# Chunked attention and a low-rank mixer on one core: side work on VectorE's queue re-spaced, transposes bound to their block, and early buffers taken from one ring of eight

## The chip, the core and the metric

The kernel runs on one core of a Trainium2 chip. A core has TensorE (PE; its weight loads are shown as PEld), VectorE (DVE), ScalarE (ACT), GpSimd (POOL) and SyncE (SP), and 16 DMA engines that they share. Each engine works through its own queue strictly in order and waits on semaphores for the others. The metric is device time in microseconds (us) of one execution, the median of several.

## The reference

```python
def _attn_ref(q, k, v):                       # (8, 8, 576, 64) each: batch, heads, rows, head width
    q_c, k_c, v_c = (a.reshape(B, H, 9, 64, D) for a in (q, k, v))
    scores = (1 / sqrt(D)) * np.matmul(q_c, k_c.transpose(0, 1, 2, 4, 3))
    attn = softmax(scores)                    # with the row maximum taken off first
    return np.matmul(attn, v_c).reshape(B, H, S, D)

def _moe_ref(x, U, V, w_ch1, w_ch2):          # x: (8, 576, 512), the attention's output, heads side by side
    h = x.transpose(0, 2, 1) @ U @ V          # rank 32, mixes the 576 rows
    u = x + h.transpose(0, 2, 1)
    return u + np.maximum(u @ w_ch1, 0.0) @ w_ch2    # 512 -> 2048 -> 512
```

The weights U, V, w_ch1 and w_ch2 arrive as 8-byte floats; the rest is fp32.

## The kernel before

**Tiles.** Two batches make a pair (pr = 0 to 3), 1152 rows, cut into nine tiles of 128 rows (t = 0 to 8). Three tiles make a group (g = 0 to 2).

**The main work.** For each pair and group, the channel product runs in 16 blocks f = 0 to 15, each over 128 of the 2048 hidden channels. `hidden` (L744) makes h in 12 matmuls of 384 columns; `relu_high` (L759, ACT) writes hh, the high part of relu(h); `relu_low` (L764, DVE) writes hl, the rest; `project_out` (L771) adds hh and hl times the second weight into o, 9 matmuls of 512 columns per block. TensorE's queue holds the `hidden` of a block ahead of the o of the block before it, sometimes two ahead. There are 192 such blocks.

**The lead-in.** Until the first block can run, the kernel turns the 8-byte weights into fp32 pairs (`rounding`, `splitting`: ACT and DVE), does the attention of pair 0's nine tiles, projects them with U (`project_ops`, y), with V (`mix_ops`, u), and transposes the sum (ut). This part and the first 32 blocks (groups 0 and 1 of pair 0) are ordered by a planner, `order` (L147), from costs and from counts of buffers, `ROOM`. V goes through `v_ops` (L273): loaded to `vraw`, rounded in `vroom` by six DVE steps (L94 to L103), written to DRAM as `vrows` (POOL queue, L290), read back four times as `vall` (POOL queue, L295), then split into `vst` by ACT (L298) and DVE (L303). The v rows of each early tile (`qkv_t`) are also loaded from POOL's queue.

**The steady part.** From pair 0, group 2 on, side work for the next tiles is called from a list of words (`LATER`, `FIRST`, L951) spread evenly over the 4 places of each of the 16 blocks, but for the last `TAIL` places. The words: `t` the two transposes of q and k of a tile, `s` its scores and softmax, `q` the transpose of the softmax's result, `l`, `f`, `u` the three steps of the mixer for a tile, `p` a projection step, `h` one strided copy of q or k within DRAM (halfq, halfk), `.` nothing. Where a word is called doesn't fix where its instructions stand: the framework's scheduler puts each engine's instructions in order by its own estimate, within the data dependencies.

**Transposes through DMA and DVE.** From pair 1's tile 2 on no TensorE transpose is used. q and k come by one DMA in 32-row blocks (qn, kn; L417) and are turned by DVE block transposes into qT and kT (`squares`, L480). The softmax result ex is written to DRAM (es_td, L459), read back (es, L400) and turned into eT (`square_e`, L539). The mixer's x goes the same way: us_td (L454), us (L400), uT (`square_u`, L709). scores (sc) read qT and kT; `values` (av) reads eT; ACT and DVE split uT into uth and utl, the next group's input.

**Buffers.** `slot` (L71) gives out buffers by tag: three of "qk", two of "vn", one each of "e", "eT", "us", "uT". The early tiles take ex from "qk" and eT from "eT", "us", "uT" in turn (L467); the last three weights' rooms take `XTAGS` (L53). The load of a tile (`load`, L446) is called in the word `s` of the tile before it, right behind that tile's scores (L941 to L945).

Of the kernel before, what the change touches and what calls it, by code (L numbers as in the profile page):

```python
# [12 lines left out]
U32 = mybir.dt.uint32  # L13
# [8 lines left out]
def kernel(  # L22
# [29 lines left out]
    XROOM = 3  # L52
    XTAGS = (("qk", "us"), ("qk", "uT"), ("qk", "e"))  # L53
    BLOCKS = [(hp, e, c) for hp in range(HP) for e in range(2) for c in range(2)]
# [13 lines left out]
    def bank(name):  # L68
        return psum.tile([P, 512], F32, tag="bank", name=name)

    def slot(tag, dtype, name, shape=(P, 512)):  # L71
        return work.tile(list(shape), dtype, tag=tag, name=name, bufs=SLOTS[tag])

# [48 lines left out]

    ROOM = {"bank": 8, "w": NF, **SLOTS, "x": NX, "y": 2, "ut": 2, "h": 2, "mx": 2, "sm": 2}
    COLD = 1.0
# [197 lines left out]
    def w_ops(f, after=None):  # L322
        st = {}

        def load():
            raw = wslot((2 * DM, 2), U32, f"wraw_{f}")
            nc.sync.dma_start(
                raw[:, 0:DM].rearrange("p (cc f) w -> p cc (f w)", cc=NCC),
                moe_w_ch1[:, 2 * f * P : 2 * (f + 1) * P].rearrange("(cc p) f -> p cc f", p=P),
            )  # L330
            nc.sync.dma_start(raw[:, DM:].rearrange("p c w -> p (c w)"), moe_w_ch2[f * P : (f + 1) * P, :])
            st["raw"] = raw

        n = 1 if f < NF - XROOM else 2
        size = 2 * DM // n
        ld = Op("SP", 3.2, load, after, take="w", lat=2.0)
        halves = []
        for z in range(n):
            cols = slice(z * size, (z + 1) * size)

            def room(z=z):
                return wslot((size,), U32, f"wroom_{f}") if n == 1 else slot(XTAGS[f - NF][z], U32, f"wroom_{f}_{z}")

            def high(v, cols=cols):
                if cols.start == 0:
                    del st["raw"]
                    w = st["w"] = wslot((2, 2 * DM), F32R, f"w_{f}")
                    w1[f] = w[:, :, 0:DM].rearrange("p s (c f) -> p s c f", c=NCC)
                    w2[f] = w[:, :, DM:]
                nc.scalar.copy(st["w"][:, 0, cols], v)  # L350

            def low(v, cols=cols):
                nc.vector.tensor_sub(st["w"][:, 1, cols], v, st["w"][:, 0, cols])

            raw = Later(lambda cols=cols: st["raw"][:, cols])
            tag = "w" if n == 1 else XTAGS[f - NF][z]
            halves.append((*rounding(raw, room, ld, tag, size), high, low, tag))
        rounded = [h[0] for h in halves]
        return [splitting(r, high, low, rounded, tag, size) for _, r, high, low, tag in halves]
# [90 lines left out]
    def put(src, name, by_channel=False):  # L450
# [9 lines left out]
        return kept  # L460

    def attention_ops(pr, t, *after):
        n = f"{pr}_{t}"
        st = {}
        mine = early(pr, t)
        own = plain(pr, t)
        tag_e, tag_eT = ("qk", ("eT", "us", "uT")[t % 3]) if mine else ("e", "eT")  # L467

# [9 lines left out]
        def squares(z, name):  # L478
            dst = slot("qk", F32, name + n, (P, HP, P))
            nc.vector.transpose(  # L480
                dst.rearrange("p h (n j a) -> p n a h j", n=2, j=SQ),
                loaded[pr, t][z].rearrange("p (n a) (h i) -> p n a h i", n=2, i=SQ),
            )
            st[name] = dst
# [52 lines left out]
        def square_e():  # L537
            st["eT_"] = slot("eT", F32, "eT_" + n, (P, HP, P))
            nc.vector.transpose(  # L539
                st["eT_"].rearrange("p h (j a) -> p a h j", j=SQ), st["es"].rearrange("p a (h i) -> p a h i", i=SQ)  # L540
# [136 lines left out]
    def mix_ops(pr, t, x, ys, after=None, first=None):  # L677
# [29 lines left out]
        def square_u():  # L707
            uT = st["t"] = slot("uT", F32, "uT_" + n)
            nc.vector.transpose(  # L709
                uT.rearrange("p (c j a) -> p a c j", c=NCC, j=SQ), st["us"].rearrange("p a (c i) -> p a c i", i=SQ)  # L710
# [124 lines left out]
    GATES = (28, 30)  # L835
    TAIL = 8
    HALVES_FROM = 13
# [90 lines left out]

    def begin_next(i):
        if i + 1 < len(tiles) and tiles[i + 1] not in loaded:  # L930
            load(*tiles[i + 1])

    def attend(pr, t, what):
# [9 lines left out]
        done = behind.pop(0)[2] if len(behind) > 1 else []  # L943
        i = tiles.index((pr, t))
        return [*done, soft[0], lambda: begin_next(i), *soft[1:]]  # L945

    def do(group):
# [3 lines left out]
    LATER = {  # L951
# [3 lines left out]
    }  # L955
    FIRST = "t2 s2 p0 p1 h h t3 q2 s3 p2 h . h t4 q3 s4 p3 h . t5 h q4 s5 p4 . l0 . f0 l1 . . u0 f1 l2 . . u1 f2 . . . u2"

# [7 lines left out]
    def go(pr, g, word):  # L965
        if word == ".":
            return
        if word == "h":
            if to_halve:
                to_halve.pop(0)()  # L970
            return
        kind, i = word[0], int(word[1:])
        if kind in "tsqa":
            at = pr + 1 if g else pr
# [66 lines left out]
```

## Time and profile before

| | |
|---|---|
| time, median of 3 runs | 1000.47 us (999.69 to 1002.86) |
| the profiled execution: its time, its span in the trace | 1000.45 us, 998.6 us |
| TensorE busy / weight loads / DVE / ACT | 944.5 / 821.2 / 486.7 / 213.2 us |
| granted TensorE clock, mean | 0.98 |
| first matmul of the first block | at 70.8 us |

All positions are us from the span's start. In a row of the timeline stand start, length, engine, line, operation, output<-input with shapes, the count of instructions merged, and in brackets how long the engine sat idle before and what ended that. "SPq" and "POOL ... DMA_DIRECT2D" rows are issues of DMAs; their length is the time to issue. A row of the table by windows gives busy time and count of PE, PEld, DVE, ACT, POOL, then the granted clock (1.00 is full), the DMA share and GB/s. A row of the waits gives total, times and longest, in us. "issue" as a releaser means that the profile shows nothing that was waited for.

### The profile page before, as it was taken

What the parts mean: (1) busy time and instruction counts of PE and PEld (TensorE: products, weight loads), DVE (VectorE), ACT (ScalarE), POOL (GpSimd) and SP (SyncE); (2) the same over time, 40 slices, a digit from 0 to 9 for tenths busy, and PEclk for the clock granted to TensorE, in tenths of its full rate; (3) what the DMA queues carried; (4) which work ended last, traced back from release to release, by engine and by line L of the source; (5) the groups of instructions that cost most, each with busy time, mean ns of one, the idle gap of its engine ahead of it and who ended that gap; (6) DMA issues with size and microseconds to landing.
All of it is one profiled execution on the core that took longest, in us unless ns stands there. A gap on an engine that the chain in (4) does not pass through costs nothing.

```text
span 998.6 us, 16154 instructions
## 1 busy us (share of the span) xinstructions
PE 944.5 (95%) x6660; PEld 821.2 (82%) x6663; DVE 486.7 (49%) x915; ACT 213.2 (21%) x385; POOL 33.8 (3%) x89
## 2 busy tenths in 40 slices
PE   7969999998998999999999799999999999999998
PEld 4648999877797888888898689787888788899997
DVE  5869999673544534443544443453443553421211
ACT  4433433231111212111211111111111121111110
POOL 6510000000000000000000000000000000000000
PEclk8979999999999899999999899999999999999999
DMA  9952178657526524544643632663231412210000
GB/s 223 246 150 81 53 179 189 98 148 147 129 61 141 110 63 102 120 96 106 131 86 75 132 76 43 140 128 88 83 81 39 125 45 43 75 22 1 32 1 32
DMA packets 272152, 97.80 MB, mean 98 GB/s; under 512 B 224192, under 2 KB 258016, under 8 KB 272080
## 3 DMA queue, kind: packets, MB, share of 16 engines
q1 hardware_dynamic: 270560, 93.61, 41.4%
q0 software_dynamic: 1520, 3.17, 1.4%
q8 instruction: 52, 0.85, 0.4%
q14 instruction: 20, 0.16, 0.0%
HBM read 73.61 MB, written 37.30 MB: 111 GB/s over the span
## 4 chain that ended last, share of the span: by engine, by line
PE 72%; DMA 13%; SPq 5%; DVE 5%; issue 2%; ACT 2%; POOL 1%; DVEq 0%; POOLq 0%; ACTq 0%
PE o L779 32%; PE h L752 32%; SPq L438 3%; DMA kn<-halfk 2%; PE av L550 2%; PE sc L502 1%; DVE eT L539 1%; SPq L454 1%; DMA es_2d<-ex 1%; PE u L687 1%; DMA us_3d<-x 1%; DMA es<-es_2d 1%; DMA us<-us_3d 1%; SPq L417 1%; DMA vall<-vrows 1%
## 5 line engine op out<-in xcount | busy, mean ns | idle before, releaser
L752 PE MATMUL h<-uth,w 128*128 128x384 f32 x1536 | 413.2, 339 | 0.0
L779 PE MATMUL o<-w,hh 128*128 128x512 f32 x1152 | 357.8, 400 | 3.3 <-ACT hh L761 3.3
L752 PEld LDWEIGHTS h<-uth,w 128*128 128x128 f32 x1536 | 281.5, 188 | 8.6
L752 PE MATMUL h<-utl,w 128*128 128x384 f32 x768 | 259.8, 338 | 0.0
L779 PEld LDWEIGHTS o<-w,hh 128*128 128x128 f32 x1152 | 214.4, 190 | 43.2 <-ACT hh L761 5.3
L779 PE MATMUL o<-w,hl 128*128 128x512 f32 x576 | 219.6, 402 | 3.5 <-DVE hl L766 3.3
L766 DVE SCALAR_TENSOR_TENSOR hl<-h,hh 128x384 fp32r<-128x384 f32 x192 | 104.9, 551 | 209.7 <-ACT hh L761 209.2
L761 ACT ACTIVATE hh<-h 128x384 fp32r<-128x384 f32 x192 | 93.8, 490 | 437.1 <-PE h L752 436.9
L752 PEld LDWEIGHTS h<-utl,w 128*128 128x128 f32 x768 | 144.5, 188 | 7.1
L779 PEld LDWEIGHTS o<-w,hl 128*128 128x128 f32 x576 | 108.8, 190 | 33.1 <-DVE hl L766 7.7
L539 DVE STREAM_TRANSPOSE eT<-es 128x512 f32<-128x512 f32 x25 | 27.4, 1096 | 84.1 <-DMA es<-es_3d 14.6
L709 DVE STREAM_TRANSPOSE uT<-us 128x512 f32<-128x512 f32 x27 | 29.6, 1097 | 60.9 <-DMA us<-us_2d 12.6
L719 ACT CAST uth<-uT 128x512 fp32r<-128x512 f32 x27 | 16.8, 620 | 124.5 <-DVE uT L709 124.5
L693 DVE TENSOR_TENSOR x<-u,x 128x512 f32<-128x512 f32 x36 | 24.1, 682 | 32.6 <-PE u L687 32.5
L531 ACT ACTIVATE ex<-ex 128x512 f32<-128x512 f32 x36 | 22.7, 632 | 79.3 <-DVE ex L523 72.8
L480 DVE STREAM_TRANSPOSE kT<-kn 128x512 f32<-128x512 f32 x25 | 17.8, 712 | 41.2 <-DMA kn<-halfk 41.2
L550 PEld LDWEIGHTS av<-vn,eT 64*64 64x64 f32 x864 | 17.3, 133 | 25.0 <-issue 25.0
L550 PE MATMUL av<-vn,eT 64*64 64x65 f32 x864 | 21.9, 224 | 13.5 <-DVE eT L539 8.8
L636 ACT CAST xh<-x 128x512 fp32r<-128x512 f32 x30 | 18.6, 619 | 61.4 <-DVE x L569 55.5
L516 DVE TENSOR_REDUCE mx<-sc 128x4 f32<-128x256 f32 x72 | 28.0, 416 | 4.9 <-PE sc L502 4.8
L414 POOL MEMSET vn<- 128x8 f32 x27 | 3.0, 114 | 737.1 <-PE av L550 720.7
L569 DVE TENSOR_TENSOR x<-av,sm 128x256 f32<-128x256 f32 x72 | 27.2, 419 | 1.2
(95 smaller groups left out, 562.3 us busy)
## 6 DMA issues: line engine op xcount, KB each, us to landing
wraw<-in_moe_w_ch_dram SPq DMA_DIRECT2D x32, 512.0 KB
out_dram<-x SPq DMA_DIRECT2D x36, 256.0 KB
halfq<-in_q_dram SPq DMA_DIRECT2D x24, 288.0 KB
halfk<-in_k_dram SPq DMA_DIRECT2D x24, 288.0 KB
vn<-in_v_dram SPq DMA_DIRECT2D x108, 64.0 KB
qn<-halfq SPq DMA_DIRECT2D x25, 256.0 KB
kn<-halfk SPq DMA_DIRECT2D x25, 256.0 KB
qkv<-in_v_dram POOLq DMA_DIRECT2D x36, 64.0 KB, 6.0
```

What stands on the lines that cost most here:

```text
L438: d = queue.dma_start(vn[e * C : (e + 1) * C, c, :, 0:D], v[b, heads(pr, t, e), s0 : s0 + C, :].rearrange("h s d -> s h d"),)
L516: nc.vector.reduce_max(mx, st["sc"][e], axis=AX.X)
L531: nc.scalar.activation(exf, exf, AF.Exp, scale=SCALE)
L539: nc.vector.transpose(st["eT_"].rearrange("p h (j a) -> p a h j", j=SQ), st["es"].rearrange("p a (h i) -> p a h i", i=SQ))
L550: nc.tensor.matmul(ps[e][cs, hp * D1 : (hp + 1) * D1], lhsT=st["eT_"][rows, hp, cs], rhs=vn[rows, c, hp, :], start=True, stop=True,)
L569: nc.vector.tensor_mul(by_head[:, heads(pr, t, e), :], st["av"][e][:, :, 0:D], st["sm"][:, e].unsqueeze(2).broadcast_to([P, HP, D]),)
L693: nc.vector.tensor_add(x, st["u"], x)
L709: nc.vector.transpose(uT.rearrange("p (c j a) -> p a c j", c=NCC, j=SQ), st["us"].rearrange("p a (c i) -> p a c i", i=SQ))
L752: o = nc.tensor.matmul(ps[:, :GN], lhsT=w[:, z, cc], rhs=u[:, cc, :], start=(n == 0), stop=(n == 3 * NCC - 1))
L761: nc.scalar.activation(hh, ps[:, :GN], AF.Relu)
L766: nc.vector.scalar_tensor_tensor(hl, ps[:, :GN], 0.0, hh, op0=ALU.max, op1=ALU.subtract)
L779: nc.tensor.matmul(acc[g, j], lhsT=h[:, js], rhs=w2[f][:, z], start=(first and i == 0), stop=(final and i == 2),)
```

## The change

Four things are changed. (1) In the planned part, the early tiles' ex and eT and the last three weights' rooms take a buffer from one ring of eight in a fixed turn (`RING`), and the planner counts them as one stock "slot" of eight. (2) Every DVE block transpose gets an added dependency on the last matmul of the `hidden` issued last when it is called (`square`), so that the scheduler can't set it ahead of that block. (3) Loads of tiles leave the word `s` and get a word of their own, `n`, with numbers from 9 on meaning the next pair. (4) The lists are spaced anew, and `TAIL` is 6 in place of 8: 58 of 64 places are used, not 56.

```diff
-    XTAGS = (("qk", "us"), ("qk", "uT"), ("qk", "e"))
+    RING = ("qk", "qk", "qk", "e", "eT", "us", "uT", "vn")
...
+    turn_of = itertools.cycle(RING)
+
     def slot(tag, dtype, name, shape=(P, 512)):
+        tag = next(turn_of) if tag == "slot" else tag
         return work.tile(list(shape), dtype, tag=tag, name=name, bufs=SLOTS[tag])
...
-    ROOM = {"bank": 8, "w": NF, **SLOTS, "x": NX, "y": 2, "ut": 2, "h": 2, "mx": 2, "sm": 2}
+    ROOM = {"bank": 8, "w": NF, **SLOTS, "slot": len(RING), "x": NX, "y": 2, "ut": 2, "h": 2, "mx": 2, "sm": 2}
...
-                return wslot((size,), U32, f"wroom_{f}") if n == 1 else slot(XTAGS[f - NF][z], U32, f"wroom_{f}_{z}")
+                return wslot((size,), U32, f"wroom_{f}") if n == 1 else slot("slot", U32, f"wroom_{f}_{z}")
...
+    def square(dst, src):
+        turned = nc.vector.transpose(dst, src)
+        sync = mybir.DependencyInfo(mybir.DependencyClass.Sync, mybir.DependencyReason.DATA)
+        tc.add_manual_dep(turned.ins, hidden_last[-1].ins.name, sync, reason="not before this block")
...
-        tag_e, tag_eT = ("qk", ("eT", "us", "uT")[t % 3]) if mine else ("e", "eT")
+        tag_e, tag_eT = ("slot", "slot") if mine else ("e", "eT")
...
-            nc.vector.transpose(
+            square(
...
-    TAIL = 8
+    TAIL = 6
...
-        i = tiles.index((pr, t))
-        return [*done, soft[0], lambda: begin_next(i), *soft[1:]]
+        return [*done, *soft]
...
     LATER = {
-        0: "t6 q5 s6 l3 h f3 h t7 q6 s7 u3 p0 p1 h t8 h q7 s8 p2 p3 h . . q8 a8 p4 . l4 . f4 l5 . . u4 f5 . . . u5",
+        0: "t6 q5 s6 l3 n7 h f3 t7 q6 s7 u3 n8 p0 h t8 q7 s8 p1 n9 h p2 h q8 a8 p3 h p4 . l4 . f4 l5 . u4 f5 . u5",
...
+        if kind == "n":
+            key = pr + (g > 0) + i // NT, i % NT
+            if key[0] < NPAIR:
+                load(*key)
+            return
```

The three calls of `nc.vector.transpose` (L480, L539, L709 before) all go through `square`. The line numbers of the changed kernel are higher by up to 9, so L480, L539 and L709 are one line there, L467.

**VectorE, pair 1, group 0, blocks 1 to 3.** qT_7 and kT_7 are the transposes of tile 7, eT_6 that of tile 6's softmax, uT_3 that of tile 3's x; hl_0_f is the low part of block f of group 0. Before:

```order
L480 STREAM_TRANSPOSE qT_7_3196<-qn_7_3106 128x2x2x4x32
L523 TENSOR_TENSOR ex_6_3116<-sc_1_6_3088,mx_6_3117 128x4x2x32
L523 TENSOR_TENSOR ex_6_3116<-sc_1_6_3089,mx_6_3117 128x4x2x32
L791 TENSOR_TENSOR x_8_772<-o_8_2382,x_8_772 128x512
L480 STREAM_TRANSPOSE kT_7_3198<-kn_7_3107 128x2x2x4x32
L693 TENSOR_TENSOR x_3_2587<-u_3_3149,x_3_2587 128x512
L766 SCALAR_TENSOR_TENSOR hl_0_1_3147<-h_0_1_3132,hh_0_1_3145 128x384
L766 SCALAR_TENSOR_TENSOR hl_0_2_3187<-h_0_2_3172,hh_0_2_3185 128x384
L539 STREAM_TRANSPOSE eT_6_3203<-es_6_3125 128x4x128
L709 STREAM_TRANSPOSE uT_3_3292<-us_3_3170 128x4x128
L766 SCALAR_TENSOR_TENSOR hl_0_3_3220<-h_0_3_3205,hh_0_3_3218 128x384
```

and now:

```order
L532 TENSOR_TENSOR ex_6_3113<-sc_1_6_3095,mx_6_3114 128x4x2x32
L578 TENSOR_TENSOR x_5_3092<-av_1_5_3070,sm_5_3088 128x256
L578 TENSOR_TENSOR x_5_3092<-av_1_5_3071,sm_5_3088 128x256
L532 TENSOR_TENSOR ex_6_3113<-sc_1_6_3096,mx_6_3114 128x4x2x32
L702 TENSOR_TENSOR x_3_2615<-u_3_3141,x_3_2615 128x512
L775 SCALAR_TENSOR_TENSOR hl_0_1_3139<-h_0_1_3124,hh_0_1_3137 128x384
L467 STREAM_TRANSPOSE qT_7_3197<-qn_7_3157 128x2x2x4x32
L775 SCALAR_TENSOR_TENSOR hl_0_2_3187<-h_0_2_3172,hh_0_2_3185 128x384
L467 STREAM_TRANSPOSE kT_7_3199<-kn_7_3158 128x2x2x4x32
L467 STREAM_TRANSPOSE eT_6_3221<-es_6_3122 128x4x128
L467 STREAM_TRANSPOSE uT_3_3286<-us_3_3192 128x4x128
L775 SCALAR_TENSOR_TENSOR hl_0_3_3219<-h_0_3_3204,hh_0_3_3217 128x384
```

The pair qT_7, kT_7 stood inside and behind tile 6's softmax and ahead of hl_0_1; now each stands one block later, qT_7 behind hl_0_1 and kT_7 behind hl_0_2. eT_6 and uT_3 stand ahead of hl_0_3 as before.

**SyncE, the same place.** kn_7 is tile 7's load of k, es_6d and es_6 are the store and the read-back of tile 6's softmax, us_3d and us_3 those of tile 3's x. Before:

```order
L417 DMA kn_7_3107<-halfk_1574 128x2x256
L438 DMA vn_7_3108<-in_v_dram 64x4x64 x2
L794 DMA out_dram<-x_8_772 128x512
L459 DMA es_6d<-ex_6_3116 128x4x128
L389 DMA halfk_2641<-in_k_dram 9x256x32
L454 DMA us_3d<-x_3_2587 128x4x32 x3
L400 DMA es_6_3125<-es_6d 128x512
L454 DMA us_3d<-x_3_2587 128x4x32
L417 DMA qn_8_3265<-halfq_1400 128x2x256
L400 DMA us_3_3170<-us_3d 128x512
```

and now:

```order
L803 DMA out_dram<-x_8_775 128x512
L421 DMA kn_7_3158<-halfk_1574 128x2x256
L442 DMA vn_7_3159<-in_v_dram 64x4x64 x3
L458 DMA us_3d<-x_3_2615 128x4x32
L463 DMA es_6d<-ex_6_3113 128x4x128
L458 DMA us_3d<-x_3_2615 128x4x32 x3
L404 DMA es_6_3122<-es_6d 128x512
L404 DMA us_3_3192<-us_3d 128x512
L421 DMA qn_8_3312<-halfq_1442 128x2x256
```

The strided copies halfk have left this stretch, the store us_3d begins ahead of es_6d, and us_3 follows es_6 with nothing between.

**GpSimd's queue in the lead-in.** Rows qkv_t load the v rows of early tile t. Before:

```order
L438 DMA qkv_2_347<-in_v_dram 64x4x64 x4
L414 MEMSET qkv_8_500 128x8
L438 DMA qkv_5_434<-in_v_dram 64x4x64 x4
L290 DMA vrows<-vroom 128x144
L438 DMA qkv_8_500<-in_v_dram 64x4x64 x4
L414 MEMSET qkv_6_636 128x8
L295 DMA vall<-vrows 32x576 x4
L414 MEMSET qkv_7_706 128x8
L438 DMA qkv_6_636<-in_v_dram 64x4x64 x4
```

and now:

```order
L442 DMA qkv_2_347<-in_v_dram 64x4x64 x4
L418 MEMSET qkv_8_483 128x8
L294 DMA vrows<-vroom 128x144
L442 DMA qkv_5_432<-in_v_dram 64x4x64 x4
L299 DMA vall<-vrows 32x576 x4
L442 DMA qkv_8_483<-in_v_dram 64x4x64 x4
L418 MEMSET qkv_6_622 128x8
L418 MEMSET qkv_7_682 128x8
L442 DMA qkv_6_622<-in_v_dram 64x4x64 x4
```

vrows is now ahead of tile 5's loads and vall ahead of tile 8's. On VectorE the six steps on vroom are now in one piece, where before the last three stood behind the softmax of tile 2 and the end of tile 4.

More of the change, by code (lines that the diff above doesn't have):

```diff
@@ L1 @@
+import itertools
 import math
@@ L355, in w_ops @@
             raw = Later(lambda cols=cols: st["raw"][:, cols])
-            tag = "w" if n == 1 else XTAGS[f - NF][z]
+            tag = "w" if n == 1 else "slot"
             halves.append((*rounding(raw, room, ld, tag, size), high, low, tag))
@@ L538, in square_e @@
             st["eT_"] = slot("eT", F32, "eT_" + n, (P, HP, P))
-            nc.vector.transpose(
+            square(
                 st["eT_"].rearrange("p h (j a) -> p a h j", j=SQ), st["es"].rearrange("p a (h i) -> p a h i", i=SQ)
@@ L708, in square_u @@
             uT = st["t"] = slot("uT", F32, "uT_" + n)
-            nc.vector.transpose(
+            square(
                 uT.rearrange("p (c j a) -> p a c j", c=NCC, j=SQ), st["us"].rearrange("p a (c i) -> p a c i", i=SQ)
@@ L927 @@
     behind = []
-    def begin_next(i):
-        if i + 1 < len(tiles) and tiles[i + 1] not in loaded:
-            load(*tiles[i + 1])
     def attend(pr, t, what):
@@ L951 @@
     LATER = {
[3 rows of a table removed]
[3 rows of a table added]
     }
-    FIRST = "t2 s2 p0 p1 h h t3 q2 s3 p2 h . h t4 q3 s4 p3 h . t5 h q4 s5 p4 . l0 . f0 l1 . . u0 f1 l2 . . u1 f2 . . . u2"
+    FIRST = "p0 p1 h t2 s2 n3 h . t3 . q2 s3 p2 n4 h h . t4 . q3 s4 p3 n5 h . t5 . q4 s5 h n6 p4 . l0 . f0 l1 . u0 f1 l2 . u1 f2 . . u2"
     def plan():
```

4 rows, old and new, of the table LATER are left out of this document.

## The prediction

> **What bounds the kernel now.** I read the table by windows first, to see where TensorE stands still, then the waits of TensorE, then the timeline at one long stop, then the clock.
>
> ```profile
> 78.00:200.00 122.00, 121.77 (x613) 109.96 (x611) 109.98 (x148) 44.12 (x65) 0.00 (x0) 1.00 0.54 115
> 200.00:994.00 794.00, 762.56 (x5259) 670.74 (x5259) 322.87 (x639) 134.80 (x260) 2.81 (x25) 0.99 0.37 84
> ```
>
> TensorE is the bound: of the 122 us from 78 to 200 it idles 0.2. From 200 on it idles 794 - 762.56 = **31.4 us**, and more in the lead-in ahead of 78. VectorE, busy 323 of those 794 us, isn't full; it is late at certain points. The waits of TensorE from 200 to 830:
>
> ```profile
> PE y L647 <- ACT xh L636: 9.8, 3, 3.9
> PE av L550 <- DVE eT L539: 8.8, 5, 3.4
> PE av L550 <- issue: 4.6, 3, 2.3
> ```
>
> The columns are total, times, longest. These rows name 23.2 of the 31.4 us: products of y and av that wait for data which came through DMA and a VectorE transpose. Most of the rest are o products behind hh and hl, which queue behind such a transpose. The timeline of the stop near 320 us (pair 1, group 0) shows how: VectorE, ScalarE, SyncE's queue and TensorE.
>
> ```profile
> 305.89 0.75 DVE L516 TENSOR_REDUCE mx<-sc 128x4 f32<-128x256 f32 x2
> 306.56 0.70 DVE L480 STREAM_TRANSPOSE qT<-qn 128x512 f32<-128x512 f32 x1
> 307.18 0.71 DVE L523 TENSOR_TENSOR ex<-sc,mx 128x256 f32<-128x256 f32 x2
> ...
> 311.57 0.71 DVE L480 STREAM_TRANSPOSE kT<-kn 128x512 f32<-128x512 f32 x1 [3.08 <-DMA kn<-halfk]
> ...
> 319.38 1.08 DVE L539 STREAM_TRANSPOSE eT<-es 128x512 f32<-128x512 f32 x1 [5.59 <-DMA es<-es_6d]
> 322.24 1.08 DVE L709 STREAM_TRANSPOSE uT<-us 128x512 f32<-128x512 f32 x1 [1.79 <-DMA us<-us_3d]
> 323.18 0.54 DVE L766 SCALAR_TENSOR_TENSOR hl<-h,hh 128x384 fp32r<-128x384 f32 x1
> ```
>
> ```profile
> 307.93 0.63 ACT L531 ACTIVATE ex<-ex 128x512 f32<-128x512 f32 x1 [5.17 <-DVE ex L523]
> ```
>
> ```profile
> 308.42 0.60 SPq L417 DMA_DIRECT2D kn<-halfk  x1
> ...
> 311.07 0.38 SPq L459 DMA_DIRECT2D es_6d<-ex  x1
> ...
> 316.36 0.47 SPq L400 DMA_DIRECT2D es<-es_6d  x1
> ...
> 319.75 0.33 SPq L400 DMA_DIRECT2D us<-us_3d  x1
> ```
>
> ```profile
> 320.55 0.70 PE L550 MATMUL av<-vn,eT 64*64 64x65 f32 x32 [1.52 <-issue]
> ...
> 325.40 0.80 PE L647 MATMUL y<-xh,ust 128*128 128x512 f32 x1 [3.69 <-ACT xh L636]
> ```
>
> The scores of tile 6 reach VectorE at 305.89. The transpose qT of the next tile is set into the softmax, then kT stands 3.08 us for a load issued at 308.42, and all behind it is late: the add to x that us_3d stores, so that the store, the read-back issued at 319.75 and uT (322.24) slip. The softmax, ready at 308.56, is stored only at 311.07, behind kn and vn on SP's queue, and read back at 316.36. So eT ends at 320.46, 14.6 us after the scores came; av waits 1.52 us and y 3.69. The row of y counts three such stops, one for each pair that has a next one.
>
> ```profile
> DVE kT L480 <- DMA kn<-halfk: 41.2, 21, 5.7
> ```
>
> Waits for kn were 21, with 41.2 us, most of them hidden by the `hidden` that TensorE runs ahead.
>
> **The change part by part.** Steady part, idle time. No transpose and no DMA is added or taken away. The added dependency makes a transpose wait for the `hidden` of its block; hl of that block can't start before that either, and in the new order none stands ahead of the hl of an earlier block, so the wait by itself costs nothing. I walked the place above through the new order with the rows' durations, and these of the chain of waits:
>
> ```profile
> 78.78 4.22 PE h L752 x24
> 83.00 4.18 PE o L779 x18
> ...
> 229.98 3.05 DMA es_2d<-ex
> 233.04 2.55 DMA es<-es_2d
> ```
>
> A block's 12 h are 2.11 us, its 9 o 2.09. From the end of tile 6's scores to its av TensorE now has three blocks of these, u (a matmul of an o's size, 0.2) and six more o (1.4): 14.2 us; before it was 13.5, with the stop of 1.52 behind. VectorE does the maxima and differences without qT between (0.3 + 0.75 + 0.71, and 0.8 for the scaling of tile 5 among them), exp takes 0.63, the store waits for one issue of us_3d on SP (0.5), is issued (0.38) and lands (3.05), the read-back takes 2.55, eT 1.08: 10.8 us, 3.4 ahead of av. uT_3, whose store is no longer behind a kT, ends at about 14.9, hl_0_3 at 15.5; it is wanted at 17.5, and y, placed one h later than before, at 18. So the 5.2 us of this place go, and those of its two likes. For av of tiles 2 and 8 the same count gives 13.0 and 11.8 us from scores to av where it gave 11.4 and 9.6, against stops of 8.8 us in five, the longest 3.4. The o rows go with the kT that leaves their way. What I leave: three places in each of three pairs have under 1 us of room by the same walk (eT_7, eT_8, uT_5); with 0.8 us each and some contention that is **8 us**. So 31.4 - 8 = **23.4 us less**. Bounds: 31.4 less; or, if all 41.2 us of the kT row came through to TensorE, 41.2 - 31.4 = 9.8 more.
>
> Steady part, clock. The windows behind the stops, and one with a shorter stop:
>
> ```profile
> 236.00:242.00 6.00, 5.04 (x76) 4.66 (x77) 4.81 (x13) 1.25 (x2) 0.11 (x1) 0.72 0.64 114
> 321.00:327.00 6.00, 2.31 (x55) 1.89 (x45) 3.71 (x9) 1.85 (x3) 0.11 (x1) 0.70 0.76 160
> 327.00:333.00 6.00, 6.00 (x25) 5.21 (x24) 3.48 (x8) 1.08 (x3) 0.00 (x0) 0.73 0.38 103
> 560.00:566.00 6.00, 3.68 (x9) 3.00 (x10) 4.95 (x14) 1.85 (x3) 0.00 (x0) 0.52 0.61 120
> 796.00:802.00 6.00, 3.96 (x10) 2.91 (x11) 5.07 (x14) 2.40 (x5) 0.00 (x0) 0.72 0.36 87
> 676.00:686.00 10.00, 7.88 (x96) 6.57 (x95) 2.25 (x6) 0.98 (x2) 0.09 (x1) 1.00 0.27 80
> ```
>
> The granted clock is the figure behind POOL's count. Busy time times what is missing: 5.04 x 0.28 + 2.31 x 0.30 + 6.00 x 0.27 + 3.68 x 0.48 + 3.96 x 0.28 = **6.6 us**. The last row holds a stop of 2.1 us at 1.00. I take the loss to shrink as the long stops do: 5.6 of 6.6 us go; bounds 0 and 6.6. The Trainium skill (TensorE: Matmul & The Clock Gate, What's actually happening) says the clock falls to half only after an idle window of about 3.4 us; by it none would be left with stops under 1 us, which is 1 us less than my sum.
>
> Lead-in: VectorE on V, POOL's queue, ScalarE, TensorE, and the windows.
>
> ```profile
> 32.05 0.31 DVE L98 SCALAR_TENSOR_TENSOR vroom<-vraw,vroom 128x144 uint32<-128x144 uint32 x1
> ...
> 36.38 0.23 DVE L101 TENSOR_SCALAR vraw<-vroom 128x144 uint32<-128x144 uint32 x1
> ...
> 36.99 0.31 DVE L103 TENSOR_TENSOR vroom<-vroom,vraw 128x144 f32<-128x144 f32 x1
> ```
>
> ```profile
> 37.59 0.56 POOL L290 DMA_DIRECT2D vrows<-vroom  x1 [3.47 <-DVE vroom L103]
> ...
> 44.19 1.03 POOL L295 DMA_DIRECT2D vall<-vrows  x2 [3.41 <-issue]
> 45.40 1.46 POOL L295 DMA_DIRECT2D vall<-vrows  x2 [0.18 <-issue]
> ```
>
> ```profile
> 53.87 0.67 ACT L298 CAST vst<-vall 128x576 fp32r<-128x576 f32 x1 [7.35 <-DMA vall<-vrows]
> ```
>
> ```profile
> 58.59 2.05 PE L687 MATMUL u<-ys,vst 128*128 128x512 f32 x4 [7.27 <-DVE vst L303]
> ```
>
> ```profile
> 50.00:58.00 8.00, 1.33 (x7) 0.50 (x5) 1.83 (x4) 3.44 (x6) 2.61 (x6) 0.73 1.09 272
> 58.00:64.00 6.00, 5.41 (x60) 4.14 (x64) 3.88 (x7) 1.27 (x3) 0.00 (x0) 0.50 0.24 67
> ```
>
> V's rounding is split: its first three steps end at 32.36, its last three (36.38 to 37.30, 0.9 us) stand behind other work. vrows is issued at 37.59, the read-back vall from 44.19 to 46.86, it lands at 53.85, and TensorE stands 7.3 us; then the clock is 0.50 with 5.41 us busy, 2.7 us lost. Now the six steps are in one piece and end at 32.36 + 0.9 = 33.3. vrows goes there and lands some 3.6 us later (0.56 to issue, 3.05 as the stores above); vall, behind tile 5's loads alone, is issued from 36.9 to 39.5 and with the same 7 us lands at about **46.5**, 7.3 us earlier. What is late next is VectorE: it was idle 8.00 - 1.83 and 6.00 - 3.88, together 8.3 us, from 50 to 64, and needs perhaps 2.3 of it still for the chain from scores over softmax to av of tiles 6 and 7. So **6 us less**; bounds 0 and 8.3. That passes on only as far as VectorE's weight steps come earlier too, since it is busy 110 of 122 us from 78 to 200; they stand behind the same hole, so I take it whole. The ring costs no instruction; what it frees (the rooms of the last weights) lies where TensorE has 0.2 us to win.
>
> The wider spacing puts the last u of a group later; its uT must end ahead of the next group's first h. By the lengths above that chain is 10 us (add 0.7, four stores 2, landing 3, read-back 2.9, turn 1.1), and by the order it has 14 or more: nothing.
>
> **Sum.** From the span 998.6: - 23.4 - 5.6 - 6.0 = 963.6; the execution took 1.85 us more than its span (1000.45, the median to 0.02 us), so 965.5, **966 us**.
>
> **The rivals.** The stops move. The stores and read-backs keep their length, and half of the 23.2 us of av and y stays beside my 8, that is 11.6 us, with 3 us of the clock: 966 + 14.6 = **980 us**. For it: the room found is 1 to 4 us, and every landing in it is from one execution. Against it: no transpose stands inside a softmax any more. Chance 0.20.
>
> The lead-in doesn't gain. vall then starts among the loads for which the DMA column shows 1.09 up to 58, and lands no earlier than they let it: 966 + 6 = **972 us**. For it: that column is 0.24 only from 58 on, just behind vall's landing. Against: the same 7 us were measured among those loads. Chance 0.10. The Trainium skill speaks for this rival (DMA: Bandwidth & Descriptors, Issuing engines are not separate DMA queues): what POOL issues runs on the same 16 DMA engines as what SP issues, and another queue saves only the time to issue.
>
> Slower. A load now goes out one block (4.2 us) ahead of its turn, not two, since `n` stands a word or more behind `s`. Should kn land behind its own block's hh, VectorE stands at kT ahead of the hl that TensorE wants next, with nothing run ahead to hide it. For 24 tiles this decides from 35.0 / 24 = 1.5 us per tile on; with 1.8, below the 41.2 / 21 = 2.0 that VectorE stood there on average, the time is 966 + 43 = **1009 us**. Against it: kn is issued about 2.2 us behind the scores and lands 3.7 later (0.60 + 3.08), at 6; kT of tile 7 stands behind hl_0_2, at 8. Chance 0.07.
>
> No change. The order moves, but av, y and o wait for the same last DMAs and the lead-in for its weights: **998 us**, 0.05.
>
> **How the numbers follow.** My forecast has 0.58; its own range is 958 to 974. With the first two rivals that is 0.88, so the range goes from 955 (all terms at their better bounds: 1000.5 - 31.4 - 6.6 - 8.3 = 954.2) to 984, past the first rival. A measurement tells about 0.3%, 3 us, from no change: faster 0.88, same 0.05, slower 0.07.
>
> **What would show it.** Right: in the changed profile TensorE idles under 12 us from 190 on, no row of y behind xh is above 1 us, the row of kT behind kn is far under 41 us, the granted clock has no window under 0.9 after 100 us; ACT waits under 2 us for vall and the first h stands near 65, not 70.8. Wrong: rows of eT or uT with TensorE's av, y or o behind them as large as now; a wait for vall of 5 us or more; or kT behind kn at 40 us, with o waiting on it.

## The result and the profile after

The changed kernel takes **950.54 us** (median of 4 runs, 949.43 to 953.01), against 1000.08 (994.17 to 1002.86, 4 runs) for the one before: a ratio of **0.9516**, 95% interval 0.9469 to 0.9562. The forecast was 966, its range 955 to 984. The forecast was wrong in size: the kernel did get faster, at the place that was named, but the gain came out 15 us larger than forecast and beyond the range. The profiled execution of the changed kernel took 949.43 us, its span 947.7 in place of 998.6.

First the table by windows of the changed kernel, for the lead-in, the blocks that the planner ordered, and the steady part (columns as above; PE's busy time is the second figure):

```profile
50.00:58.00 8.00, 8.00 (x107) 4.48 (x104) 5.22 (x12) 2.08 (x4) 1.01 (x2) 0.79 1.06 279
58.00:64.00 6.00, 4.80 (x80) 3.00 (x79) 5.80 (x14) 2.85 (x4) 0.11 (x1) 1.00 0.89 309
...
200.00:830.00 630.00, 626.95 (x4655) 556.96 (x4654) 296.45 (x597) 120.48 (x228) 2.84 (x25) 1.00 0.45 103
```

and the same stretch of the steady part before:

```profile
200.00:830.00 630.00, 598.89 (x4446) 523.34 (x4447) 285.04 (x577) 112.96 (x216) 2.81 (x25) 0.98 0.44 99
```

From 200 to 830 TensorE stood still for 630 - 598.89 = 31.1 us before, and for 3.05 now. The hole of the lead-in at 50 to 58 is full of work. The waits of TensorE from 190 to 830 in the changed kernel (total, times, longest):

```profile
PE av L559 <- DVE eT L467: 1.6, 3, 0.9
PE ps_qT L481 <- DMA qn<-in_q_dram: 1.6, 1, 1.6
PE ps_kT L481 <- DMA kn<-in_k_dram: 0.9, 1, 0.9
```

The row of y behind xh (9.8) is gone, and so are the waits of o behind hh and hl. VectorE's group of kT in the table by lines, whose last figures are its idle time and what ended it:

```profile
L467 DVE STREAM_TRANSPOSE kT<-kn 128x512 f32<-128x512 f32 x25 | 17.2, 690 | 0.4 <-DMA kn<-halfk 0.4
```

41.2 us are now 0.4. Last, the place that the prediction walked, pair 1, group 0, now near 300 us; TensorE, VectorE, ScalarE and SyncE's queue in the timeline:

```profile
294.31 0.69 PE L511 MATMUL sc<-kT,qT 64*64 64x64 f32 x32
309.22 0.70 PE L559 MATMUL av<-vn,eT 64*64 64x65 f32 x32
```

```profile
296.08 0.41 DVE L525 TENSOR_REDUCE mx<-sc 128x4 f32<-128x256 f32 x1
...
301.71 0.71 DVE L467 STREAM_TRANSPOSE qT<-qn 128x512 f32<-128x512 f32 x1 [2.44 <-PE h L761]
302.34 0.52 DVE L775 SCALAR_TENSOR_TENSOR hl<-h,hh 128x384 fp32r<-128x384 f32 x1
302.79 0.69 DVE L467 STREAM_TRANSPOSE kT<-kn 128x512 f32<-128x512 f32 x1
306.98 1.09 DVE L467 STREAM_TRANSPOSE eT<-es 128x512 f32<-128x512 f32 x1 [3.50 <-DMA es<-es_6d]
308.28 1.09 DVE L467 STREAM_TRANSPOSE uT<-us 128x512 f32<-128x512 f32 x1 [0.21 <-DMA us<-us_3d]
```

```profile
298.24 0.63 ACT L540 ACTIVATE ex<-ex 128x512 f32<-128x512 f32 x1 [0.43 <-DVE ex L532]
```

```profile
298.95 1.98 SPq L442 DMA_DIRECT2D vn<-in_v_dram  x3
301.03 0.55 SPq L458 DMA_DIRECT2D us_3d<-x  x1
301.68 0.45 SPq L463 DMA_DIRECT2D es_6d<-ex  x1
```

No transpose stands inside the softmax, and neither qT nor kT waits for its load. From the end of the scores (295.00) to av TensorE has 14.2 us of other work, to the tenth what the walk had. eT ends at 308.07, after 13.1 us, not 10.8: the store es_6d, ready at 298.87, still stood 2.8 us behind three loads of v and a store on SP's queue (301.68 against 298.87). The stop is gone, with 1.1 us of room, not 3.4.

### The profile page after: what moved, and what is told of

It is laid out like the page before. It is cut to its first block, busy times and chain, and to the rows that moved or that the text cites. A ratio compares the mean times of both kernels' runs of the same rounds, so it can differ in the third digit from the quotient of the medians.

```text
span 947.7 us, 16187 instructions
## 1 busy us (share of the span) xinstructions
PE 922.5 (97%) x6665; PEld 808.8 (85%) x6665; DVE 483.3 (51%) x915; ACT 215.4 (23%) x385; POOL 33.0 (3%) x89
## 4 chain that ended last, share of the span: by engine, by line
PE 82%; DMA 7%; DVE 5%; SPq 2%; issue 2%; ACT 2%; POOL 0%; DVEq 0%; POOLq 0%; ACTq 0%
PE h L761 38%; PE o L788 37%; DMA qkv<-in_v_dram 2%; PE sc L511 2%; PE av L559 2%; DMA es_7d<-ex 1%; DMA us<-us_3d 1%; DMA es<-es_7d 1%; PE u L696 1%; DMA us_3d<-x 1%; DVE eT L467 1%; DMA uraw<-in_moe_U_dram 1%; PE y L663 1%; PE y L657 1%; PE y L656 1%
## 5 line engine op out<-in xcount | busy, mean ns | idle before, releaser
L788 PE MATMUL o<-w,hh 128*128 128x512 f32 x1152 | 347.8, 393 | 0.0
L788 PE MATMUL o<-w,hl 128*128 128x512 f32 x576 | 214.8, 395 | 0.0
L467 DVE STREAM_TRANSPOSE uT<-us 128x512 f32<-128x512 f32 x27 | 29.6, 1097 | 48.0 <-PE h L761 24.0
L467 DVE STREAM_TRANSPOSE eT<-es 128x512 f32<-128x512 f32 x25 | 26.9, 1077 | 44.5 <-DMA es<-es_6d 11.3
L467 DVE STREAM_TRANSPOSE qT<-qn 128x512 f32<-128x512 f32 x25 | 17.7, 709 | 49.7 <-PE h L761 48.0
L578 DVE TENSOR_TENSOR x<-av,sm 128x256 f32<-128x256 f32 x72 | 27.2, 418 | 1.1
L649 DVE TENSOR_TENSOR xl<-x,xh 128x512 fp32r<-128x512 f32 x30 | 20.6, 685 | 10.6 <-ACT xh L645 9.8
L559 PEld LDWEIGHTS av<-vn,eT 64*64 64x64 f32 x864 | 15.5, 133 | 12.0 <-issue 12.0
```

The lines of the kernel that those rows point to most:

```text
L467: turned = nc.vector.transpose(dst, src)
L559: nc.tensor.matmul(ps[e][cs, hp * D1 : (hp + 1) * D1], lhsT=st["eT_"][rows, hp, cs], rhs=vn[rows, c, hp, :], start=True, stop=True,)
L578: nc.vector.tensor_mul(by_head[:, heads(pr, t, e), :], st["av"][e][:, :, 0:D], st["sm"][:, e].unsqueeze(2).broadcast_to([P, HP, D]),)
L649: nc.vector.tensor_sub(st["l"], x_of[pr, i + 4 * e], st["h"])
L788: nc.tensor.matmul(acc[g, j], lhsT=h[:, js], rhs=w2[f][:, z], start=(first and i == 0), stop=(final and i == 2),)
```

## The experiments

They ran on three chips, each kernel with runs of the one before beside it, whose median lay between 995.9 and 999.6; ratios are to those runs. Where two kernels from different chips differ by a few us, their profiles are compared too. Where TensorE has no gap, a "block" below is 12 h and 9 o; its length is read from VectorE's hl in the last group, 15 blocks from first to last start.

**The two kernels again**, for one number of the traces that nothing in the prediction covers. Unedited.

> The kernel before, looked at once more for one thing: how long TensorE takes for a block where it has no gap. In the last group a block of 12 h and 9 o took 4.205 us in the first profile of before (31 blocks, 16 of them at 4.20 to 4.21) and 4.145 in the changed kernel, both at a granted clock of 1.00; over the 1000 us that is some 12 us which are neither idle time nor lost clock. Theory A, the rate belongs to the execution or its chip: here, on one chip with the changed kernel, both take the same, and before comes out near 988. Theory B, it belongs to the kernel: 4.205 here again, and about 1000.

> The changed kernel, beside the run above on the same chip. Theory A: its block in the gapless tail is as long as that of before on this chip, within 0.01 us. Theory B: 4.145 here against 4.205.

1002.93 and 951.26 us. Blocks as in the first profiles, 4.207 and 4.147 us: the rate belongs to the kernel, not to the execution. The rows of hl that give it, from the first profile of the kernel before:

```profile
L766 DVE SCALAR_TENSOR_TENSOR hl<-h,hh x16: 557/558/560, 918.5 to 981.6; 128x384 fp32r<-128x384 f32 x16
```

and from that of the changed kernel:

```profile
L775 DVE SCALAR_TENSOR_TENSOR hl<-h,hh x16: 557/558/559, 868.7 to 930.9; 128x384 fp32r<-128x384 f32 x16
```

The last two times in a row are the starts of the first and the last: 63.1 / 15 and 62.2 / 15.

**The binding alone, and the change without it.** In before, at its three places (squares, square_e, square_u):

```diff
-            nc.vector.transpose(
+            square(
```

> Before with the binding of the block transposes alone: old buffers, old lists, old loads. VectorE's order at pair 1, group 0 is then that of the changed kernel (qT behind hl_0_1, kT behind hl_0_2). Theory 1, the transposes set into softmaxes made the stops: nearly the whole steady gain, 25 to 35 us less than before, and the row of kT behind kn goes from 41 us to under 5. Rival, the lists and the loads at their own word make the room: 0 to 10 us less, the y and av rows stay at 15 us or more.

and in the changed kernel, at the same three, the other way round:

```diff
-            square(
+            nc.vector.transpose(
```

> The changed kernel without the binding: new lists, new loads, ring. kT stands behind the softmax's differences again, ahead of the add to x and of hl_0_1. Theory 1: 25 to 35 us slower than the changed kernel, with stops of 3 us at av and y. Rival: at most 10 us slower. A third case, slower than before: loads that now go out later make kT wait longer than it did, above 1000 us.

Binding alone: 981.7 us, ratio 0.9825 (0.9807 to 0.9843). Without it: 987.96, 0.9879 (0.9856 to 0.9902). The binding alone brings 18 us, between the theory and its rival; to take it out costs 37, more than either said. The waits of TensorE from 190 to 830 with the binding alone:

```profile
PE av L555 <- DVE eT L463: 7.1, 2, 4.0
PE y L652 <- ACT xh L641: 7.0, 3, 2.7
```

and with the new lists and the ring, but unbound:

```profile
PE h L756 <- DVE hl L770: 13.4, 5, 3.3
PE o L783 <- DVE hl L770: 4.0, 4, 2.0
```

With the binding alone the transposes stand right, yet av and y come early for their stores and read-backs. With the lists unbound these have their time, but a kT that waits for its load (38.5 us in all in its group) holds up the hl queued behind it, and h and o wait for that. Each part takes away one kind of stop and leaves the other.

**The place of the operands.** The ring also shifts, in the program's allocation, what is allocated behind it: ys, uth, utl, hh and hl, the operands of the main work beside the weights w. An unused tile moves them alone.

```diff
+            if not padded:
+                padded.append(work.tile([P, 16], F32, tag="pad", name="pad", bufs=1))
             y = work.tile([P, DM], F32R, tag="y", name=f"ys_{pr}_{e}", bufs=2)
```

(16 floats are 64 bytes; other sizes likewise.)

> Before with one unused tile of 64 bytes per partition allocated ahead of ys; nothing else is edited. The operands behind it (ys, uth, utl, hh, hl, in the program's addresses) move from 32 to 96 bytes past a multiple of 128, where the changed kernel has them; the weights w stay at 32. Two kernels with the old buffers (before, its binding alone) take 4.206 us for a gapless block, two with the ring (the changed kernel, the same without its binding) 4.147. Theory, the ring changed the rate by these addresses: 4.147 here, and the time falls by 1.2 to 1.5%, 12 to 15 us, with the stops left as they are. Rival, the rate comes of something else in the ring's code (order in the lead-in, rooms of weights): 4.206, time the same within 3 us.

> The changed kernel with the same unused tile of 64 bytes ahead of ys, which puts the operands back at 32 bytes past a multiple of 128. Theory of addresses: 4.206 for a gapless block, 10 to 14 us slower than the changed kernel, near 963. Rival: 4.147 and 950.

> The changed kernel with 32 bytes: the operands at a multiple of 128, the weights at 32. If only the distance between operands and weights counts (64 is good, 0 is bad), the rate lies at or between 4.147 and 4.206; if a multiple of 64 or 128 is better by itself, it is under 4.147.

> The changed kernel with 96 bytes: the operands at 64 past a multiple of 128, the weights at 32. Read as the run before: under 4.147 if a multiple of 64 helps by itself, 4.147 to 4.206 if the distance counts.

Before with 64 bytes: 992.72 us, ratio 0.9961 (0.9934 to 0.9988), and its row of hl reads 62.2 us for 15 blocks, 4.147:

```profile
L769 DVE SCALAR_TENSOR_TENSOR hl<-h,hh x16: 557/558/559, 911.7 to 973.9; 128x384 fp32r<-128x384 f32 x16
```

So the place sets the rate. Of the 12 to 15 us that I expected in the time only about 4 came (the profiled spans are 990.7 against 998.6 and 1001.0 us in the two profiles of before). Why it is not more is open. The profile shows no stop that grew: from 200 to 830 TensorE idles 27.2 us there, against 31.1 and 28.1, and the clock, summed as in the next section, takes 10.6 us, against 7.5 and 12.5. The changed kernel with 64 bytes: 953.25 (0.9551, 0.9512 to 0.9590) and a block of 4.187, not 4.206, so the rule was not yet right; 32 and 96 bytes: 954.25 and 957.54 in one execution each, 4.173 and 4.193.

**Its rule.** One tile ahead of all allocations moves weights and operands together; three more sizes move the operands alone.

```diff
+    const.tile([P, 16], F32, name="shift")
     ident = const.tile([P, P], F32, name="ident")
```

> The changed kernel with an unused tile of 64 bytes ahead of everything the kernel allocates: weights and operands move together, from 416 and 96 bytes past a multiple of 512 to 480 and 160. Theory, the distance between weights and operands sets the rate (192 bytes modulo 512 in the changed kernel): 4.147 for a gapless block, as there. Rival, the place of the operands themselves sets it: 4.187, as with 64 bytes ahead of the operands alone, which put them at 160 too.

> 128 bytes ahead of the operands alone: a distance of 320 modulo 512 (measured so far: 128 gave 4.206, 192 gave 4.147, 224 gave 4.173, 256 gave 4.187, 288 gave 4.191 us for a block). If the pattern repeats every 128 bytes: 4.147. If it is wider: another value, over 4.147 by up to 0.06, or under it.

> 192 bytes: a distance of 384. If the pattern repeats every 128 bytes: 4.187; every 256: 4.206, as the 128 of before. Under 4.147 would make a faster kernel than the changed one.

> 320 bytes: a distance of 0 modulo 512. If two reads from the same place disturb each other, this is the slowest, 4.206 or more; if the pattern repeats every 256 bytes, 4.187 as for a distance of 256. Under 4.147 would make a faster kernel than the changed one.

All blocks measured, by the distance from w to the operands in bytes, modulo 512 (each from the row of hl of its profile):

| distance | block, us | kernels |
|---|---|---|
| 0, 256 | 4.187 | 320 and 64 bytes |
| 32 (288) | 4.193 | 96 bytes |
| 64 (320) | 4.180 | 128 bytes |
| 128 (128, 384) | 4.207 | before, its binding alone, the change without the ring; 192 bytes |
| 192 | 4.147 | the change, 64 bytes in before, both moved together, the change without the binding; of the kernels below, the old lists, TAIL 8, TAIL 4, and the old buffers with 64 bytes |
| 224 | 4.173 | 32 bytes |

Moved together the block stays 4.147: the distance counts, not the place. 0 and 256 agree, and 128 and 384, which fits a pattern that repeats every 256 bytes; no other such pair was tried. No distance tried is better than the one that the change has. The four executions of this round took 952.79 to 957.18 us. The one with both moved took 955.09 although its blocks are the fast ones: its first h came only at 69.5 us, where the changed kernel's first profile has 66.8.

**The ring alone, and the change without it.** Both edits are the ring's lines of the diff above, put in or taken out.

> Before with the ring alone (old lists, old loads, no binding). The unused tile in before shortened the gapless block from 4.206 to 4.147 us and the profiled span by 8 to 10 us. Theory, the ring is worth that and 3 to 4 us of the lead-in (hl of the first block at 72.3 instead of 75.6 in the changed kernel): 8 to 13 us less than before, gapless block 4.147, first h near 67, 25 to 31 us of idle time from 200 to 830 as before. Rival: the lead-in gains only where VectorE is freed by the other parts too; first h stays near 71 and 6 to 9 us are left.

> The changed kernel with the old buffers in the lead-in. Theory: 8 to 13 us slower, 959 to 964, gapless block 4.206, first h near 70.8; idle time from 200 to 830 stays at 3 us, since the ring has no part in it. Rival: rooms freed earlier also carry the steady part; then stops come back and it is 970 or more.

Ring alone: 994.45 us, 0.9965 (0.9939 to 0.9991), about 4 us and less than the 8 to 13 expected, as with the 64 bytes. The first h is at 67.4, as the theory has it. (Its profiled execution, 1002.3 us, ran at a granted clock of at most 0.95 nearly throughout, so its block and its idle time aren't compared.) Without the ring: 957.69 us (955.51 to 959.67), 0.9581 (0.9541 to 0.9621): 7 us slower than the changed kernel, block 4.207, first h at 70.6, and no stop has come back:

```profile
200.00:830.00 630.00, 626.92 (x4658) 555.69 (x4659) 298.24 (x601) 121.76 (x229) 2.84 (x25) 1.00 0.45 104
```

**The lists of before with binding and ring, and the spacing.** In the changed kernel LATER, FIRST and begin_next are put back, and TAIL is 8; one of the lists:

```diff
-        1: "l6 t0 f6 s0 l7 n1 u6 f7 h t1 q0 s1 l8 n2 u7 f8 h t2 q1 s2 h n3 h u8 t3 . q2 s3 h n4 . .",
+        1: "l6 t0 f6 s0 l7 h u6 f7 h t1 q0 s1 l8 u7 f8 h t2 h q1 s2 u8 h . . t3 q2 s3 . .",
```

> The changed kernel with the lists of before: old words and spacing, loads begun behind each tile's first step, TAIL 8; binding and ring stay. The binding alone brought 18 us of idle time and clock (982 against 1000), the new lists without binding, with the ring, 988, little more than the ring's share: alone they bring next to nothing. Theory, the two need each other (lists make the room only when no transpose stands in a softmax): 968 to 973 here, with y behind xh and av behind eT at 6 us each again. Rival, the effects add: 952 to 957.

Then the changed kernel with this line alone; a further kernel has TAIL = 4.

```diff
-    TAIL = 6
+    TAIL = 8
```

> The changed kernel with TAIL 8, so all words of a list stand a little closer. The prediction put the wider spacing at nothing, since the last chain of a group has 14 us for 10: 950 within 2 us. Rival: the places with under 1 us of room by the walk (eT_7, eT_8, uT_5) come late by the 0.2 us or so that a word stands earlier, and 3 to 6 us of stops come back.

> The changed kernel with TAIL 4: words stand wider still. TAIL 8 cost 15 us by stops at av in the first groups of two pairs; if the room still falls short at the places where 3 us of idle time are left between 200 and 830, up to 2 us less than the changed kernel; if the last word of a group now comes too late for the next group's first h, 5 us or more slower, with h waiting for utl.

The old lists: 978.58, 0.9788 (0.9754 to 0.9822). To put the old lists back costs 28 us here, where the binding stands; without the binding the new lists brought at most 9 (0.9879 against the ring's 0.9965). So each needs the other, as the theory had it; but 978.58 is only 3 us under the binding alone, and I had expected 968 to 973, too much for the ring. This run puts back the words, their spacing and the place of the loads together; of the three only the spacing was also tried alone. TAIL 8: **966.04** (962.0 to 967.86), 0.9660 (0.9622 to 0.9699), 15.5 us slower than the changed kernel. In its profiled execution (962.0 us) TensorE idles 12.6 us from 200 to 830 instead of 3.05, and the clock takes 3.0; three stops at av make 10.0 of the 12.6. SyncE's queue at one of them, pair 1's tile 8, with the softmax on ScalarE and av on TensorE:

```profile
326.96 2.88 SPq L393 DMA_DIRECT2D halfq<-in_q_dram  x1
329.94 3.58 SPq L442 DMA_DIRECT2D vn<-in_v_dram  x2
333.61 0.55 SPq L421 DMA_DIRECT2D kn<-halfk  x1
334.22 1.26 SPq L442 DMA_DIRECT2D vn<-in_v_dram  x2
335.58 0.55 SPq L463 DMA_DIRECT2D es_8d<-ex  x1
```

```profile
329.20 0.63 ACT L540 ACTIVATE ex<-ex 128x512 f32<-128x512 f32 x1 [4.29 <-DVE ex L532]
```

```profile
341.92 1.27 PE L559 MATMUL av<-vn,eT 64*64 64x65 f32 x32 [3.59 <-issue]
```

The softmax is ready at 329.83, but its store goes out at 335.58, behind a strided copy and loads of the next tile. In the changed kernel the same loads are out earlier:

```profile
325.84 1.14 SPq L421 DMA_DIRECT2D kn<-halfk  x1
327.04 1.26 SPq L442 DMA_DIRECT2D vn<-in_v_dram  x2
328.40 0.55 SPq L463 DMA_DIRECT2D es_8d<-ex  x1
```

There the softmax ends at 327.57 (326.94 + 0.63), and the store follows within 0.9 us. Tile 8 of the next pair has the same stop with TAIL 8, 3.38 us. TAIL 4: 952.55, 0.9567 (0.9543 to 0.9591), no better than 6.

**The rate without the ring's lead-in.** The old buffers, and the 64 bytes.

> The changed kernel with the old buffers in the lead-in, and 64 unused bytes ahead of ys, which give the operands the distance of 192 that the ring gives them. What is left between this and the changed kernel is the ring's order of the lead-in alone. Theory, the lead-in is worth 3 to 4 us: gapless block 4.147, first h near 70.8, time 953 to 955. Rival, the whole of the 7 us that the old buffers cost is the rate: 950 to 951. Third, the lead-in's 6 us of the prediction: 956 or more, where the rate would have cost little.

949.72 us (949.38 to 951.48), 0.9536 (0.9514 to 0.9558), block 4.147: the changed kernel's time within the runs' spread, though its first h stands at 70.5, not 66.8. The rival holds. Against the old buffers without the 64 bytes, idle time from 200 to 830 is the same (3.30 and 3.08 us) and nothing is lost to the clock there; the first hl starts at 74.8 in both, the last at 939.6 instead of 947.4. So the rate alone is worth about 8 us. The kernel is as fast as the changed one and no faster; no kernel tried beats that by more than the spread.

## Why the prediction was right, and where it was wrong

The steps that failed, in the prediction's terms: "The ring costs no instruction ...", which gave the ring no worth beyond the lead-in (7.8 us went there); "That passes on ... I take it whole" (6.0 us forecast, 0.4 kept); "What I leave", sized at 8 us (3.05 measured); and a term that the sum didn't have, 7.2 us of busy time beside the stops, whose cause stays open. The spans of the profiled executions add up in three steps, each between two kernels: binding and lists 998.6 to 955.9 (42.7), the place of the operands 955.9 to 948.1 (7.8), the ring's lead-in 948.1 to 947.7 (0.4).

| term | forecast, us | what went, us |
|---|---|---|
| idle time of the steady part | 23.4 | 28.0 |
| clock of the steady part | 5.6 | 7.5 |
| busy time beside the stops, steady part | not in the sum | 7.2 (cause argued) |
| place of the operands (ring) | not in the sum | 7.8 |
| lead-in (ring) | 6.0 | 0.4 |
| together | 35.0 | 50.9 |

The range ended at 955 because its lower end took the three forecast terms at their best and had no other term. Each step is between single executions: the second profile of before has a span of 1001.0, and the last step, 0.4, is within the spread.

**Idle time of the steady part: mechanism right, size too small.** The stops went where the prediction said and for its reason. The mis-sized term is "What I leave", put at 8 us of 31.4: 3.05 are left from 200 to 830, so 28.0 went for 23.4 (25.0 by the second profile of before). The walk was good on TensorE (14.2 us for 14.2) and 2.3 us short on SP's queue.

**Clock: right in kind, the price of a stop too low.** Summed over windows of 2 us (busy time times what is missing of the granted clock), before lost 7.5 us from 200 to 830, the changed kernel nothing, and in its first profile no such window after 80 us is under 0.97; the sum had 5.6 of 6.6. The price is not a fixed one: in its second profile before lost 12.5 us to the clock with 3 us less idle time. The prediction read in the Trainium skill (TensorE: Matmul & The Clock Gate, What's actually happening) that the clock falls after an idle window of about 3.4 us, so that none of the loss would be left, and from 200 on the trace of the changed kernel agrees: the longest stop there is 0.9. Ahead of 200, at the first transposes of pair 1, shorter waits were enough. In the second profile of the changed kernel two stand close together, 2.23 and 0.72 us with 0.66 us of work between them; TensorE's rows, and a window behind them:

```profile
191.90 0.66 PE L481 MATMUL ps_qT<-ident,qn 128*128 128x128 f32 x4 [2.23 <-DMA qn<-in_q_dram]
193.27 0.94 PE L481 MATMUL ps_kT<-ident,kn 128*128 128x128 f32 x4 [0.72 <-ACT qT L503]
```

```profile
194.00:196.00 2.00, 2.00 (x7) 1.61 (x6) 0.00 (x0) 0.59 (x1) 0.00 (x0) 0.50 0.28 65
```

The length of the waits doesn't decide it: with TAIL 8, 1.53 and 0.89 us at this place are followed by a window at 0.50, and in the first profile of the changed kernel 1.59 and 0.94 by none under 0.97.

Beyond idle time and clock, 7.2 us more of the 42.7 are time that the windows of before count as busy. I take them for the edges of stops, which the rows of the weight loads count and those of the matmuls miss in part: the weight loads of o behind hl waited ten times, 7.1 us in the first row below, the matmuls' row has three of those times, 3.2 us. The waits of the weight loads, and of the matmuls, of before from 190 to 830:

```profile
PEld o L779 <- DVE hl L766: 7.1, 10, 1.6
```

```profile
PE o L779 <- DVE hl L766: 3.2, 3, 1.2
```

That is an argument from these rows, which hold 3.9 of the 7.2; no run isolates it, and the cause stays open. Idle 28.0, clock 7.5 and 7.2 make the 42.7, where the prediction had 29.0; with the second profile of before in its place they are 25.0, 12.5 and 7.6, so the sum had no term for some 7 us in either.

**"The wider spacing ... nothing": wrong.** Undone, it costs 15.5 us. The step looked only at the last u of a group. What the spacing buys is elsewhere, at the stop shown above on SP's queue: the loads of the next tile are out within 0.9 us of the softmax's end, where with TAIL 8 they hold its store up for 5.8.

**"The ring costs no instruction ... where TensorE has 0.2 us to win": wrong.** It costs none, but it moves the operands, and a gapless block of the main work then takes 1.4% less. Without stops that is worth 8 us (957.69 to 949.72); with the stops of before about 4. The step counted instructions and not where their operands lie.

**Lead-in: 6 us forecast, none kept.** Its chain came as worked out. V is read back earlier, vall ends its way at 46.06 (46.5 forecast; the wait is 2.15, just over the 2 named), and the hole is closed:

```profile
46.06 0.67 ACT L302 CAST vst<-vall 128x576 fp32r<-128x576 f32 x1 [2.15 <-DMA vall<-vrows]
```

The first h stands at 66.81, not 65: v of the last early tiles, now behind vall on POOL's queue, ends a wait of 1.93 us at av. Over all profiles the gain there is real: the first h lies between 65.6 and 69.8 in the fourteen with the ring, between 70.5 and 71.6 in the six with the old buffers. The step that failed is "That passes on ... I take it whole". The window from 180 to 215 in the changed kernel:

```profile
180.00:215.00 35.00, 31.35 (x279) 25.92 (x279) 20.29 (x42) 10.73 (x20) 0.28 (x3) 1.00 0.56 116
```

and the window in the kernel with the old buffers and 64 bytes:

```profile
180.00:215.00 35.00, 34.22 (x268) 29.76 (x267) 23.70 (x49) 11.93 (x23) 0.11 (x1) 1.00 0.64 122
```

3.65 us idle against 0.78. TensorE waits for q and k of the first tile of pair 1, whose loads stand on SP's queue behind strided copies (1.6 and 0.9 us, the rows of ps_qT and ps_kT above). The issue of that load, and its user on TensorE, in the changed kernel:

```profile
184.31 2.98 SPq L428 DMA_DIRECT2D qn<-in_q_dram  x1
```

```profile
190.38 0.66 PE L481 MATMUL ps_qT<-ident,qn 128*128 128x128 f32 x4 [1.59 <-DMA qn<-in_q_dram]
```

and in the kernel with the old buffers and 64 bytes:

```profile
187.07 3.16 SPq L425 DMA_DIRECT2D qn<-in_q_dram  x1
```

```profile
194.34 0.60 PE L478 MATMUL ps_qT<-ident,qn 128*128 128x128 f32 x4
```

With the ring TensorE comes to this transpose 4.5 us after the issue begins (188.79 against 184.31), without it 7.3 us after, and the load takes 6.1. So the order that the planner makes with the ring brings the load and its user 2.8 us closer together. That TensorE is merely early, and waits for loads that keep their time, is a rival which the runs refute. In the changed kernel with everything moved by 64 bytes the first h stands only at 69.5, the load goes out at 188.15, later than with the old buffers, and TensorE waits all the same:

```profile
194.47 0.66 PE L482 MATMUL ps_qT<-ident,qn 128*128 128x128 f32 x4 [2.46 <-DMA qn<-in_q_dram]
```

In all fourteen profiles with the ring TensorE idles 3.3 to 4.5 us from 180 to 215, in the six with the old buffers 0.8 to 1.9. In ten of the fourteen the granted clock also falls to 0.50 to 0.54 behind it, in none of the six.

The first and the last of all 192 hl, in the changed kernel:

```profile
L775 DVE SCALAR_TENSOR_TENSOR hl<-h,hh x192: 517/557/560, 71.8 to 939.2; 128x384 fp32r<-128x384 f32 x192
```

and in the other:

```profile
L774 DVE SCALAR_TENSOR_TENSOR hl<-h,hh x192: 515/557/559, 74.8 to 939.6; 128x384 fp32r<-128x384 f32 x192
```

3.0 us ahead at the first, 0.4 at the last. How much an order without this stop would keep, no run shows.

**The rivals.** That the lead-in doesn't gain was true in the end, though not by the loads beside vall. The stops didn't move as long as binding, lists and spacing were together; any one taken out brought some back. The slower case didn't come: kT waits 0.4 us with loads begun later.

## What to carry to other kernels

Where several queues feed one bound engine, parts of a re-ordering can be worth far more together (42 us) than one by one (18 for the binding, at most 9 for the lists), so walk every queue that the chain crosses, the one that issues the DMAs first of all. A gain at the front is not added before the rest of the new order is followed too: it can bring a later load and its user closer together, and lose there what was won. And compare the time of gapless stretches between two profiles: a change in which no instruction differs may still show there.

## What the runs showed of the hardware that was not expected

The distance in bytes between the weights and the other operand in SBUF changes the time of this kernel's fp32 matmuls by up to 1.4% at the same granted clock: 4.147 to 4.207 us for 21 of them, as in the table, and equal at two pairs of distances 256 bytes apart. The Trainium skill (TensorE: Matmul & The Clock Gate, Step-by-step: what each phase is for) has it that loading the next weights takes no read bandwidth from the running matmul; these runs show that the two operands' places do bear on each other, and not by what means.

In one execution, the profiled one of the ring alone, a granted clock of 0.95 lengthened gapless blocks far less than by a twentieth. Its window and its hl there:

```profile
900.00:950.00 50.00, 50.00 (x252) 45.42 (x251) 8.38 (x15) 5.92 (x12) 0.00 (x0) 0.95 0.04 16
```

```profile
L770 DVE SCALAR_TENSOR_TENSOR hl<-h,hh x17: 557/558/558, 916.0 to 983.4; 128x384 fp32r<-128x384 f32 x17
```

67.4 / 16 = 4.212 us, 1.6% over the 4.147 of the other kernels with this distance.
